# Two PSUM banks copied to SBUF ahead of their additions, and the row statistics cut into smaller, earlier pieces, in a spectral-attention kernel

## The chip, the cores and the metric

One core of one Trainium2 chip. The time is device microseconds of one execution: 1813.44 us before the change, the median of three runs (1812.06 to 1814.43). All traces are of single profiled executions.

## The reference

Four layers follow one another on x (1 x 2048 x 512, fp32), each with a layer norm ahead and a residual; both attentions have the same weights.

```
x = A_x
x = x + _A_ref(_layernorm(x, axis=-1), A_dft_seq_re, A_dft_seq_im, A_dft_hid_re, A_dft_hid_im)
x = x + _B_ref(_layernorm(x, axis=-1), B_wq, B_wk, B_wv, B_wo, B_beta)
x = x + _A_ref(_layernorm(x, axis=-1), A_dft_seq_re, A_dft_seq_im, A_dft_hid_re, A_dft_hid_im)
x = x + _B_ref(_layernorm(x, axis=-1), B_wq, B_wk, B_wv, B_wo, B_beta)
```

The spectral layer computes y = Cr (xn Dr) - Ci (xn Di) with DFT matrices of 2048 x 2048 and 512 x 512. The attention splits the sequence into four segments of 512 rows and 32 heads of width 16: causal softmax within the segment, plus a read of a memory (M, z) that the segments before have filled, mixed by a gate and multiplied by wo.

## The kernel before, in words

**Stages.** The rows lie in 16 tiles of 128 rows. Spectral 1 runs to about 373 us of the trace and overlaps the start of attention 1; attention 1 ends, and spectral 2 begins, near 740 us; attention 2 takes the end. fp32 precision is reached by splitting every operand into a high and a low part (`split`, L92: ACT writes the high part `chi`, DVE subtracts to get `clo`), and each product is three matmuls, high x high, high x low, low x high (`matmul3`, L104).

**Transform one of the spectral layer** multiplies the sequence matrix by xn. It is cut into seven products named P1 to P7 per column block `tcn`, by which sums of blocks are reused. `product(tcn, name)` (L497) accumulates eight steps k into two PSUM banks `m0` and `m1` (each 128x512), and then adds or copies the banks into blocks `c` in SBUF: DVE's additions are line L520, ACT's copies L518. What each product adds is in `TERMS`: P6 is subtracted from three blocks, P5 added to two, P3 to one. In spectral 1 (`direct`), P6, P5 and P3 take turns, one step each, for tcn 1, 2 and 3, so that six banks are in use by the products; the next tcn's first matmuls need banks that the last one's additions have freed. PSUM has eight banks in one pool ("bank"). All operands of a step come from a ring of loads (`cring`, `craw`, `v_all`), are added where needed (L407, L444, L457) and split (L96 on ACT, L98 on DVE).

**Statistics of rows.** A layer norm needs mean and variance of each row (`moments`: bn_stats L132, bn_aggr L133) and then 1/sqrt(var + eps). That is a chain over three engines: `ve` on DVE (L143), a power on POOL (`r`, L145), and four small DVE instructions (`rt` three times and `row_r`, L150 to L153; `row_scale`). The normalised tile is `xn` (L166). `measure(s, i, xr)` (L199) does this for a row tile whose sum a layer has just finished, the chain for all four tiles of a segment together, after the fourth.

**The attention's `prep(s, n)`** (L679) loads two row tiles, norms and transposes them on TensorE (`xnT`). For the last segment the statistics aren't known from `measure`, so it does them itself (`row_stats`, then `row_scale`), three slots ahead of the first `xn`. In the attention DVE's largest work is the custom instruction L827, which adds the mask to the score tile `nat` and takes each row's maximum (`junk`, `mx`); TensorE's `nat`, `sT`, `pv_bank`, `pqk`, `pvv` and `po` are scores, transposed scores, values and projections.

**Spectral 2** (not `direct`) normalises its 16 tiles in pairs at slots listed by hand in `ln_at`; each pair ends in `xa` splits (L96, L98). For its last four tiles the statistics are made in `normalise` itself. `negate` (L642) then writes `minus`, -1/std of all 16 tiles, which `add_rows` (L253) needs.

**What sets the order.** Every step is a generator that is placed by hand at numbered slots (`place(order, gen, *at)`); the slots run in order, and within a slot by `order`. TensorE's instructions, ACT's high parts and bn_stats stand in program order; the rest is put in order by a scheduler's timeline when the program is built. Each engine then works through its own list in that order, waiting where an instruction's input isn't there. DMAs are issued from SP's list and, for some stores, ACT's.

Of the kernel before, what the change touches and what calls it, by code (L numbers as in the profile page):

```python
# [10 lines left out]
F32 = mybir.dt.float32  # L11
F32R = mybir.dt.float32r
BF16 = mybir.dt.bfloat16
AF = mybir.ActivationFunctionType
ALU = mybir.AluOpType
# [3 lines left out]
P = 128  # L19
S, D, H = 2048, 512, 32  # L20
DH = D // H
NSEG = 4
L = S // NSEG
NT = S // P
DT = D // P
TC = S // 512
LT = L // P
# [29 lines left out]
def spectral_infini_kernel(  # L57
# [13 lines left out]
    V, A, G, T = nc.vector, nc.scalar, nc.gpsimd, nc.tensor  # L71

    consts = ctx.enter_context(tc.tile_pool(name="consts", bufs=1))
    sb = ctx.enter_context(tc.tile_pool(name="sb", bufs=1))
# [55 lines left out]
    def moments(mv, xt):  # L130
        st = sb.tile([P, 6], F32, name="st", bufs=2)
        pin(V.bn_stats(st, xt))  # L132
        V.bn_aggr(mv, st)  # L133
# [6 lines left out]
    def inverse_roots(mv):  # L140
        n = mv.shape[1]
        ve = sb.tile([P, LT], F32, name="ve", bufs=3)[:, :n]
        V.tensor_scalar_add(ve, mv[:, :, 1], EPS)  # L143
        r = sb.tile([P, LT], F32, name="r", bufs=3)[:, :n]
        G.tensor_tensor(out=r, in0=ve, in1=half_neg[:, :n], op=ALU.pow)  # L145
        return ve, r

    def row_scale(rr, ve, r):
        t = sb.tile([P, LT], F32, name="rt", bufs=2)[:, : rr.shape[1]]
        V.tensor_tensor(out=t, in0=r, in1=r, op=ALU.mult)  # L150
        V.tensor_tensor(out=t, in0=t, in1=ve, op=ALU.mult)
        V.tensor_scalar(t, t, -0.5, 1.5, op0=ALU.mult, op1=ALU.add)
        V.tensor_mul(rr, r, t)  # L153
# [30 lines left out]
    def place(order, gen, *at):  # L184
        for t in itertools.chain(*at):
            slots.setdefault(t, []).append((order, gen))
# [9 lines left out]
    row_r = consts.tile([P, NT], F32, name="row_r")  # L196
    minus = consts.tile([P, NT], F32, name="minus")

    def measure(s, i, xr):  # L199
        moments(row_mv[:, s * LT + i], xr)  # L200
        if i == LT - 1:
            done = slice(s * LT, (s + 1) * LT)
            row_scale(row_r[:, done], *inverse_roots(row_mv[:, done]))

    def place_spectral(x_in, x_out, t0, end, ln_at, direct):
        xa, xb, xs, us, wdt, c, right, plain = ({} for _ in range(8))
# [259 lines left out]
        def block(tcn, j):  # L466
            c[tcn, j] = t = pair("c", "ut" if tcn < 2 else "wd", 8, F32)
            return t
# [28 lines left out]
        def product(tcn, name):  # L497
            ps = [bank(f"m{m}") for m in range(2)]
            for k in range(HALF):
                t = right[tcn, name, k]  # L500
                for m in range(2):
                    matmul3(
                        ps[m],
                        lambda h: left(name, k, h, m),
                        lambda h: t[h],
                        k == 0,
                        k == HALF - 1,
                    )
                if k < HALF - 1:
                    yield  # L510
            for j, base, _ in TERMS[name]:
                if base != j:
                    block(tcn, j)
            for m in range(2):
                for j, base, op in TERMS[name]:
                    dst = c[tcn, j][:, m]
                    if base is None:
                        A.activation(dst, ps[m], AF.Copy)  # L518
                    else:
                        V.tensor_tensor(out=dst, in0=c[tcn, base][:, m], in1=ps[m], op=op)  # L520
            yield

        def chained(tcn):
# [78 lines left out]
        t = start  # L602
        if direct:
            place(2, contract(0), run_from(t, 4 * HALF, 2))
            for k in range(HALF):
                place(3, read_plain(0, k), [t + 8 * k + d for d in (-12, -4, 1, 4)])
                place(3, change_rows(k), [t + 8 * k + d for d in (5, 9)])
            t += 8 * HALF
            names = "P1", "P2", "P7", "P4"
            for tcn in range(1, TC):  # L610
                for n, name in enumerate(names):
                    place(2, product(tcn, name), run_from(t + n, HALF, 4))
                for k in range(HALF):
                    place(3, read_all(tcn, k), [t + 4 * k + d for d in (-11, -6, -4, -2, -1)])
                t += 4 * HALF
            for k in range(HALF):
                place(3, join_rows(k), [t + 5 * k + d for d in (-33, -27)])
            for tcn in range(1, TC):
                for n, name in enumerate(CHAIN):
                    place(2, product(tcn, name), run_from(t + n, HALF, 3))  # L620
                for k in range(0, HALF, 2):
                    place(3, read_rest(tcn, k), [t + 3 * k + d for d in (-12, -6, -3, 0)])
                t += 3 * HALF
        else:
            SOLO = 1
            phases = [(("P1",), range(SOLO)), (("P1", "P7"), range(SOLO, TC)), (("P7", "P2", "P4"), range(SOLO)), (("P2", "P4"), range(SOLO, TC))]
            for names, tcns in phases:
                n = len(names)
                for tcn in tcns:
                    for j, name in enumerate(names):  # L630
                        place(2, product(tcn, name), run_from(t + j, HALF, n))
                    for k in range(HALF):
                        u = t + n * k
                        if n == 1:
                            place(3, read_one(tcn, k, "P1"), [u - 9, u - 4])
                        else:
                            first = n - 2
                            if first:
                                place(3, read_added(tcn, k), [u + d for d in (-10, -6, -4)])
                            place(3, read_pair(tcn, k, names[first:]), [u + first + d for d in (-10, -6, -4, -3)])  # L640
                    t += n * HALF
            def negate():  # L642
                V.tensor_scalar(minus, row_r, -1.0, None, op0=ALU.mult)
                yield

            place(3, negate(), [t - 50])
            for k in range(HALF):
                place(3, add_rows(k), [t - 48 + 6 * k, t - 44 + 6 * k])
            for tcns in (0, 1), (2, 3):
                at = {tcn: [] for tcn in tcns}  # L650
                for name, tcn in itertools.product(CHAIN, tcns):
                    at[tcn] += run_from(t, HALF)
                    for k in range(HALF):
                        place(3, read_one(tcn, k, name), [t + k + d for d in (-9, -4)])
                    t += HALF
                for tcn in tcns:
                    place(2, chained(tcn), at[tcn])
        for k in range(2 * DT):
            cc, d = k // DT, k % DT
            tag = "craw" if k < 2 else ("chi", "clo")[k % 2]  # L660
            t = end - 7 + k if k < 2 else end - 3 + (k - 2) // 2
# [13 lines left out]
    def place_attention(x_in, x_out, t0, w_at, out_at):  # L675
# [3 lines left out]
        def prep(s, n):  # L679
            xt = [load_rows(x_in[s * LT + i]) for i in n]  # L680
            yield
            mine = slice(s * LT + n[0], s * LT + n[-1] + 1)
            mv, rr = row_mv[:, mine], row_r[:, mine]
            if s == NSEG - 1:
                ve, r = row_stats(xt, mv)
            yield
            if s == NSEG - 1:
                row_scale(rr, ve, r)
            for j, i in enumerate(n):
                with behind_max():  # L690
                    xn = normal(xt[j], mv[:, j], rr[:, j : j + 1])
                yield
                if i == 0:
                    xT[s] = sb.tile([P, 2, DT, 512], F32R, name="xT", bufs=1)
                pt = bank("xnT", (P, DT, P))
                for d in range(DT):
                    T.transpose(pt[:, d], xn[:, d * P : (d + 1) * P], ident)
                sl = slice(i * P, (i + 1) * P)
                split(xT[s][:, 0, :, sl], xT[s][:, 1, :, sl], pt)
                if j + 1 < len(n):  # L700
                    yield
            yield
# [477 lines left out]
        for n in range(NSEG * USEG):  # L1180
            t = t0 + SU * n
# [5 lines left out]
        for s in range(NSEG):  # L1187
            b = t0 + SS * s
            for j in range(2):
                t = b - (43, 51, 60, 60)[s] + 5 * j  # L1190
                first = (8, 5, 3)
                place(2, prep(s, (2 * j, 2 * j + 1)), [*(t - d for d in first), t, t, t + 2])
            place(2, values(s), *([light(b - 20), light(b)] if s else [run_from(b - 18, 8), light(b - 10)]))
            place(2, alloc_out(s), [b - 13])
# [14 lines left out]
            for g in range(NG):  # L1209
                t = b + SG * g  # L1210
# [25 lines left out]
    a2 = b1 + LB - 18  # L1236
    b2 = a2 + TC * 7 * HALF + LEAD

    def w_at(b):
# [7 lines left out]
    place_attention(mids[0], mids[1], b1, w_at(b1), lambda k: b1 + LB + 11 + k // 2)  # L1247
    place_spectral(
        mids[1], mids[2], a2, b2 - LEAD,
        [((2 * j, 2 * j + 1), a2 + t) for j, t in enumerate((-40, -24, -8, 2, 24, 34, 46, 54))],  # L1250
        False,
    )
    place_attention(mids[2], out_tiles, b2, w_at(b2), lambda k: b2 + LB + 8 + k)
# [83 lines left out]
```

## Time and profile before

| | |
|---|---|
| time, median of 3 runs | 1813.44 us |
| profiled execution, its own time | 1812.16 us |
| its span, first to last instruction | 1810.4 us |
| mean granted TensorE clock | 0.994 |
| busy: TensorE, DVE, ACT, POOL | 96%, 78%, 62%, 26% |

A row of the timeline reads: start in us from the span's start, duration in us, engine, line, operation, output<-inputs with shapes, how many of the kind follow one another without a gap, and in brackets how long the engine stood idle before it and what ended that. A row of the windows gives the busy time of each engine within a stretch and the granted clock in it (PEclk, 1.00 is full speed). PEld is TensorE's weight load, which lies beside its matmuls.

### The profile page before, as it was taken

What the parts mean: (1) busy time and instruction counts of PE and PEld (TensorE: products, weight loads), DVE (VectorE), ACT (ScalarE), POOL (GpSimd) and SP (SyncE); (2) the same over time, 40 slices, a digit from 0 to 9 for tenths busy, and PEclk for the clock granted to TensorE, in tenths of its full rate; (3) what the DMA queues carried; (4) which work ended last, traced back from release to release, by engine and by line L of the source; (5) the groups of instructions that cost most, each with busy time, mean ns of one, the idle gap of its engine ahead of it and who ended that gap; (6) DMA issues with size and microseconds to landing.
All of it is one profiled execution on the core that took longest, in us unless ns stands there. A gap on an engine that the chain in (4) does not pass through costs nothing.

```text
span 1810.4 us, 32184 instructions
## 1 busy us (share of the span) xinstructions
PE 1745.1 (96%) x10192; PEld 1260.2 (70%) x10192; DVE 1404.3 (78%) x4233; ACT 1116.3 (62%) x2391; POOL 475.7 (26%) x797
## 2 busy tenths in 40 slices
PE   7999999999999999999999999999998999999998
PEld 6888777877556666665578788888875666666654
DVE  8888987764877878878877997667658788787785
ACT  3334443432877878778764765444338887867785
POOL 1000000013443445355520000000134443534442
PEclk9999999999999999999999999999999999999999
DMA  8787765355443543444566876644545344344341
GB/s 279 245 274 236 249 228 169 116 168 175 137 151 108 156 127 123 138 127 132 164 205 203 275 231 221 195 147 153 170 136 179 124 138 144 116 138 139 103 130 42
DMA packets 169498, 302.81 MB, mean 167 GB/s; under 512 B 19568, under 2 KB 70768, under 8 KB 169328
## 3 DMA queue, kind: packets, MB, share of 16 engines
q1 hardware_dynamic: 159152, 287.39, 50.0%
q10 hardware_dynamic: 10176, 13.37, 2.0%
q8 instruction: 80, 1.31, 0.3%
q14 instruction: 90, 0.74, 0.1%
HBM read 211.83 MB, written 88.08 MB: 166 GB/s over the span
## 4 chain that ended last, share of the span: by engine, by line
PE 82%; DVE 10%; DMA 3%; issue 2%; ACT 2%; POOL 0%; SPq 0%; ACTq 0%; DVEq 0%; POOLq 0%
PE m L82 25%; PE pqk L82 9%; PE y L82 8%; PE pv_bank L82 8%; PE sT L82 7%; PE nat L82 6%; PE u L82 5%; PE pvv L82 4%; PE po L82 4%; DVE junk L827 3%; DVE c L520 1%; DVE clo L98 1%; PE on L82 1%; PE pm L82 1%; PE pM L82 1%
## 5 line engine op out<-in xcount | busy, mean ns | idle before, releaser
L827 DVE CUSTOM_DVE_ANT_0 junk<-nat,mask 128x512 bf16<-128x512 f32 (+3 forms) x1024 | 496.8, 485 | 159.6 <-PE nat L82 124.7
L896 ACT ACTIVATE pT<-sT 128x512 f32<-128x512 f32 x640 | 372.1, 599 | 14.7 <-DVE sT L893 1.4
L899 POOL TENSOR_SCALAR_AFFINE_SELECT pT<-pT 128x256 f32<-128x256 f32 (+1 forms) x448 | 199.1, 458 | 470.5 <-ACT pT L896 364.1
L82 PE MATMUL m<-chi,xa 128*128 128x512 f32 x1056 | 309.9, 394 | 5.6 <-ACT chi L96 2.7
L82 PE MATMUL sT<-stkq,stkk 99*128 99x256 bf16 (+3 forms) x1024 | 248.7, 304 | 3.9 <-ACT pT L896 1.6
L82 PE MATMUL nat<-stkk,stkq 96*128 96x512 bf16 (+3 forms) x1024 | 244.9, 300 | 6.8 <-DVE mx L827 3.4
L82 PE MATMUL m<-clo,xa 128*128 128x512 f32 x720 | 232.8, 396 | 4.1 <-DVE clo L98 4.1
L895 ACT ACTIVATE sT<-sT 128x256 f32<-128x256 f32 (+1 forms) x628 | 204.6, 336 | 49.3 <-PE sT L82 47.2
L82 PEld LDWEIGHTS m<-chi,xa 128*128 128x128 f32 x1056 | 198.7, 189 | 49.2 <-ACT chi L96 3.6
L82 PE MATMUL y<-wdt,us 128*128 128x512 f32 x768 | 182.3, 391 | 0.2 <-DVE wdt L98 0.2
L82 PEld LDWEIGHTS <-stkk 99*128 99x128 bf16 x1024 | 81.4, 98 | 132.1 <-issue 118.7
L82 PEld LDWEIGHTS y<-wdt,us 128*128 128x128 f32 x768 | 143.4, 188 | 30.4 <-DVE wdt L98 0.9
L82 PEld LDWEIGHTS m<-clo,xa 128*128 128x128 f32 x720 | 135.8, 189 | 36.2 <-DVE clo L98 8.3
L96 ACT ACTIVATE chi<-cring 128x512 fp32r<-128x512 f32 (+1 forms) x138 | 100.0, 728 | 95.7 <-PE m L82 42.6
L82 PE MATMUL pv_bank<-pT,v_all 128*17 128x128 f32 (+3 forms) x2048 | 154.0, 437 | 1.3 <-POOL pT L899 1.3
L145 POOL TENSOR_TENSOR r<-ve,half_neg 128x2 f32<-128x2 f32 (+2 forms) x24 | 19.4, 810 | 481.5 <-DVE ve L143 478.6
L82 PEld LDWEIGHTS <-stkq 96*128 96x128 bf16 x1024 | 94.1, 99 | 60.1 <-issue 19.0
L82 PE MATMUL pvv<-wv,xT 128*128 128x512 f32 x384 | 127.3, 443 | 3.7 <-DVE mx L827 3.7
L82 PE MATMUL pqk<-xT,wq 128*128 128x512 f32 x384 | 129.8, 447 | 0.0
L82 PE MATMUL po<-wo,oh 128*128 128x512 f32 x384 | 123.2, 436 | 3.1 <-DVE mx L827 2.2
L82 PE MATMUL pqk<-xT,wk 128*128 128x512 f32 x384 | 123.5, 430 | 0.0
L82 PEld LDWEIGHTS pv_bank<-pT,v_all 128*17 128x17 f32 x2048 | 53.5, 97 | 90.1 <-issue 83.9
(194 smaller groups left out, 2997.3 us busy)
## 6 DMA issues: line engine op xcount, KB each, us to landing
cring<-in_ct SPq DMA_DIRECT2D x97, 256.0 KB
stkq<-scrq SPq DMA_DIRECT2D x64, 384.0 KB
stkk<-scrk SPq DMA_DIRECT2D x64, 384.0 KB
cring<-sum SPq DMA_DIRECT2D x95, 256.0 KB
xt<-mid SPq DMA_DIRECT2D x64, 256.0 KB
cring<-in_ct SPq DMA_DIRECT2D x27, 512.0 KB
mid<-xr SPq DMA_DIRECT2D x48, 256.0 KB
scrq<-parts SPq DMA_DIRECT2D x32, 384.0 KB
```

The source lines that it names most:

```text
L82: return tc.keep_in_program_order(op(*args, **kwargs))
L96: pin(A.activation(hi, src, AF.Copy, scale=scale))
L98: lo_engine.tensor_tensor(out=lo, in0=src, in1=hi.bitcast(F32), op=ALU.subtract)
L145: G.tensor_tensor(out=r, in0=ve, in1=half_neg[:, :n], op=ALU.pow)
L520: V.tensor_tensor(out=dst, in0=c[tcn, base][:, m], in1=ps[m], op=op)
L827: last_max[0] = V.tensor_tensor_reduce(junk[:, :n], src, mask[:, 512 - n :], 1.0, 3e38, ALU.add, ALU.min, dst,)
L895: A.activation(blocks, blocks, AF.Relu)
L896: A.activation(dst, ps, AF.Exp, scale=-SCALE)
L899: G.affine_select(blocks, blocks, pattern=[[0, n] for n in blocks.shape[1:-1]] + [[1, P]], compare_op=ALU.is_ge, fill=0.0, base=0, channel ...
```

## The change

Five edits:

1. In transform one of spectral 1, for tcn 1 and 2 and the products P6 and P5, ACT copies both banks into SBUF tiles `kept`, and DVE's additions read `kept` and not the banks: two places in the program with four copies each.
2. `measure` runs the chain of `row_scale` for segment 0 after every two tiles, not after four.
3. `negate` is cut in two: twelve tiles at t - 60 and four at t - 36 (before: all at t - 50).
4. `prep` of the last segment has one more step (the chain apart from the first `xn`) and starts 4 slots earlier.
5. Three of spectral 2's times of `normalise` are 2, 2 and 4 slots later.

```diff
     def measure(s, i, xr):
         moments(row_mv[:, s * LT + i], xr)
-        if i == LT - 1:
-            done = slice(s * LT, (s + 1) * LT)
+        step = LT // 2 if s == 0 else LT
+        if i % step == step - 1:
+            done = slice(s * LT + i + 1 - step, s * LT + i + 1)
             row_scale(row_r[:, done], *inverse_roots(row_mv[:, done]))
...
+            held = ps
+            if direct and tcn < TC - 1 and name in ("P6", "P5"):
+                held = [
+                    sb.tile([P, 512], F32, name="kept", tag="praw", bufs=2) if name == "P6"
+                    else sb.tile([P, 768], F32, name="kept", tag="parts", bufs=2)[:, :512]
+                    for _ in range(2)
+                ]
+                for m in range(2):
+                    A.activation(held[m], ps[m], AF.Copy)
+                pass
             for m in range(2):
                 for j, base, op in TERMS[name]:
                     dst = c[tcn, j][:, m]
                     if base is None:
-                        A.activation(dst, ps[m], AF.Copy)
+                        A.activation(dst, held[m], AF.Copy)
                     else:
-                        V.tensor_tensor(out=dst, in0=c[tcn, base][:, m], in1=ps[m], op=op)
+                        V.tensor_tensor(out=dst, in0=c[tcn, base][:, m], in1=held[m], op=op)
...
-            def negate():
-                V.tensor_scalar(minus, row_r, -1.0, None, op0=ALU.mult)
+            def negate(some):
+                V.tensor_scalar(minus[:, some], row_r[:, some], -1.0, None, op0=ALU.mult)
                 yield
-            place(3, negate(), [t - 50])
+            place(3, negate(slice(0, NT - LT)), [t - 60])
+            place(3, negate(slice(NT - LT, NT)), [t - 36])
...
             if s == NSEG - 1:
                 row_scale(rr, ve, r)
+                yield
...
-                first = (8, 5, 3)
+                first = (12, 10, 6, 3) if s == NSEG - 1 else (8, 5, 3)
...
-        [((2 * j, 2 * j + 1), a2 + t) for j, t in enumerate((-40, -24, -8, 2, 24, 34, 46, 54))],
+        [((2 * j, 2 * j + 1), a2 + t) for j, t in enumerate((-40, -24, -8, 2, 24, 36, 48, 58))],
```

TensorE's instructions stand in the same order before and after. After the diff the line numbers are higher: L98 and L166 stay, L520 becomes L531, L827 L840, L643 L654.

Three places on DVE show how the rest moves. The first is the end of transform two in spectral 1 and the first `prep` of attention 1. In these rows `st` and `row_mv` are the statistics of a row tile, `xr` a finished row tile, `us` a split of transform two, and the rows with `xt` as input are the normalised tiles 0, 1 and 2 (in the second fence 0 and 1). Before:

```order
L132 BN_STATS st_3131<-xr_3082 128x6
L151 TENSOR_TENSOR rt_3073<-rt_3073,ve_3069 128x4
L133 BN_AGGR row_mv_111<-st_3131 128x2
L152 TENSOR_SCALAR rt_3073<-rt_3073 128x4
L153 TENSOR_TENSOR row_r_112<-r_3071,rt_3073 128x4
L166 TENSOR_SCALAR xn_3114<-xt_3025,row_mv_111,row_r_112 128x512
L166 TENSOR_SCALAR xn_3181<-xt_3027,row_mv_111,row_r_112 128x512
L166 TENSOR_SCALAR xn_3231<-xt_3116,row_mv_111,row_r_112 128x512
L170 TENSOR_TENSOR xr_3135<-y_3134,xr_3135 128x512
```

After:

```order
L150 TENSOR_TENSOR rt_2977<-r_2975 128x2
L151 TENSOR_TENSOR rt_2977<-rt_2977,ve_2973 128x2
L152 TENSOR_SCALAR rt_2977<-rt_2977 128x2
L153 TENSOR_TENSOR row_r_112<-r_2975,rt_2977 128x2
L166 TENSOR_SCALAR xn_3139<-xt_3050,row_mv_111,row_r_112 128x512
L166 TENSOR_SCALAR xn_3206<-xt_3052,row_mv_111,row_r_112 128x512
L170 TENSOR_TENSOR xr_3042<-y_3041,xr_3042 128x512
L98 TENSOR_TENSOR wq_3103<-raw_3054,wq_3103 128x512
L98 TENSOR_TENSOR us_3120<-c_1338,us_3120 128x256
```

The chain covers two tiles and stands, with both `xn`, 17 rows earlier, ahead of the splits and of the sums of row tiles 2 and 3.

The second place is the `prep` of the last segment in attention 1 (attention 2 has the same). `junk,mx` are maxima of score tiles, `xn` tiles 12 and 13, `pkn` and `state0` the memory's update. Before:

```order
L151 TENSOR_TENSOR rt_7880<-rt_7880,ve_7822 128x2
L1064 TENSOR_TENSOR pkn_7856<-pM_7922,same_head_2512 128x136
L827 ISA junk_7920,mx_7759<-nat_7915,mask_2507 128x384
L827 ISA mx_7759 128x1
L152 TENSOR_SCALAR rt_7880<-rt_7880 128x2
L1071 TENSOR_TENSOR state0_4319<-state0_4319,pkn_7856 128x136
L827 ISA junk_7948,mx_7759<-nat_7946,mask_2507 128x512
L827 ISA mx_7759 128x1
L153 TENSOR_TENSOR row_r_112<-r_7824,rt_7880 128x2
L166 TENSOR_SCALAR xn_7885<-xt_7743,row_mv_111,row_r_112 128x512
L166 TENSOR_SCALAR xn_7966<-xt_7745,row_mv_111,row_r_112 128x512
```

After:

```order
L143 TENSOR_SCALAR ve_7875<-row_mv_111 128x2
L98 TENSOR_TENSOR oh_7901<-oT_7896,oh_7901 128x512
L840 ISA junk_7927,mx_7803<-nat_7922,mask_2515 128x256
L840 ISA mx_7803 128x1
L166 TENSOR_SCALAR xn_7933<-xt_7690,row_mv_111,row_r_112 128x512
L840 ISA junk_7942,mx_7803<-nat_7940,mask_2515 128x512
L840 ISA mx_7803 128x1
L150 TENSOR_TENSOR rt_7984<-r_7877 128x2
L1077 TENSOR_TENSOR pkn_7909<-pM_7966,same_head_2520 128x136
```

The first `xn` stands ahead of four maxima that stood ahead of it before; its own chain stands about 40 rows higher (between the maxima in which DVE had its last gap), and the `ve` and `rt` seen here are those of tiles 14 and 15.

The third place is the last `normalise` of spectral 2 (tiles 14 and 15), within transform one. `chi` and `clo` are the split operands of the products, in TensorE's order. Before:

```order
L143 TENSOR_SCALAR ve_11628<-row_mv_111 128x2
L150 TENSOR_TENSOR rt_11668<-r_11630 128x2
L151 TENSOR_TENSOR rt_11668<-rt_11668,ve_11628 128x2
L152 TENSOR_SCALAR rt_11668<-rt_11668 128x2
L153 TENSOR_TENSOR row_r_112<-r_11630,rt_11668 128x2
L166 TENSOR_SCALAR xn_11673<-xt_11562,row_mv_111,row_r_112 128x512
L166 TENSOR_SCALAR xn_11678<-xt_11564,row_mv_111,row_r_112 128x512
L643 TENSOR_SCALAR minus_113<-row_r_112 128x16
L98 TENSOR_TENSOR xa_11675<-xn_11673,xa_11675 128x512
L98 TENSOR_TENSOR xa_11680<-xn_11678,xa_11680 128x512
L98 TENSOR_TENSOR chi_11683<-cring_10482,chi_11683 128x512
```

After (the rows from `chi_11692` on to the block; `chi_11692` is the counterpart of `chi_11683`):

```order
L98 TENSOR_TENSOR chi_11692<-cring_10516,chi_11692 128x512
L458 TENSOR_TENSOR craw_11074<-craw_11074,cring_10516 128x512
L531 TENSOR_TENSOR c_11702<-c_11689,m1_11513 128x512
L132 BN_STATS st_11705<-xt_11640 128x6
L98 TENSOR_TENSOR clo_11715<-cring_10516,clo_11715 128x512
L98 TENSOR_TENSOR chi_11728<-cring_10516,chi_11728 128x512
L445 TENSOR_TENSOR craw_11074<-craw_11074,craw_11075 128x512
L98 TENSOR_TENSOR clo_11742<-craw_11074,clo_11742 128x512
L458 TENSOR_TENSOR cring_10516<-cring_10516,craw_11075 128x512
L133 BN_AGGR row_mv_111<-st_11705 128x2
L132 BN_STATS st_11708<-xt_11642 128x6
L133 BN_AGGR row_mv_111<-st_11708 128x2
```

The block from `ve` to the second `xa` follows right behind these rows: it now stands behind four operands of the products (`chi_11692`, `clo_11715`, `chi_11728`, `clo_11742`) that stood behind it before.

## The prediction

> **What bounds the kernel now.** I read the page's busy times first, then the waits of TensorE (PE), then the timeline around each long wait, then the windows' granted clock.
>
> ```profile
> span 1810.4 us, 32184 instructions
> PE 1745.1 (96%) x10192; PEld 1260.2 (70%) x10192; DVE 1404.3 (78%) x4233; ACT 1116.3 (62%) x2391; POOL 475.7 (26%) x797
> ```
>
> PE is busy for 96% of the span, and the change leaves its instructions as they are. So only two things can go: PE's idle 65 us, and time in which its clock is throttled. The waits of PE (total us, times, longest) say whom it waits for:
>
> ```profile
> PE xnT L82 <- DVE xn L166: 10.2, 7, 2.2
> PE m L82 <- DVE clo L98: 4.1, 5, 1.9
> PE m L82 <- ACT chi L96: 2.7, 1, 2.7
> PE m L82 <- DVE c L520: 2.1, 2, 1.6
> ```
>
> The first, third and fourth rows are the waits that the five edits touch: norms that come late, a product operand behind a norm, and banks that DVE hasn't freed. Placed in time:
>
> ```profile
> 274.07 0.61 PE L82 MATMUL m<-chi,xa 128*128 128x512 f32 x1 [1.60 <-DVE c L520]
> 309.30 0.50 PE L82 MATMUL m<-chi,xa 128*128 128x512 f32 x1 [0.46 <-DVE c L520]
> 373.65 0.63 PE L82 MATMUL xnT<-ident,xn 128*128 128x128 f32 x4 [1.82 <-DVE xn L166]
> 720.58 0.63 PE L82 MATMUL xnT<-ident,xn 128*128 128x128 f32 x4 [2.16 <-DVE xn L166]
> 1003.43 0.49 PE L82 MATMUL m<-chi,xa 128*128 128x512 f32 x1 [2.73 <-ACT chi L96]
> 1004.33 2.16 PE L82 MATMUL m<-chi,xa 128*128 128x512 f32 x5 [0.40 <-DVE chi L98]
> 1607.86 0.63 PE L82 MATMUL xnT<-ident,xn 128*128 128x128 f32 x4 [2.15 <-DVE xn L166]
> ```
>
> These stalls sum to 11.32 us. Behind four of them the clock falls; the column after POOL's busy time is the granted clock:
>
> ```profile
> 274.00:278.00 4.00, 3.93 (x10) 3.10 (x11) 3.34 (x6) 1.06 (x1) 0.00 (x0) 0.57 0.70 245
> 373.00:377.00 4.00, 3.35 (x17) 2.88 (x18) 2.40 (x5) 0.64 (x2) 0.00 (x0) 1.00 0.58 202
> 721.00:725.00 4.00, 4.00 (x21) 2.34 (x23) 3.97 (x12) 2.57 (x5) 2.36 (x3) 0.57 0.73 229
> 1003.00:1008.00 5.00, 4.17 (x11) 3.04 (x12) 5.00 (x10) 5.00 (x10) 0.00 (x0) 0.68 0.70 230
> 1608.00:1613.00 5.00, 5.00 (x31) 2.67 (x34) 4.93 (x15) 2.57 (x5) 2.46 (x3) 0.66 0.69 223
> ```
>
> A clock of 0.57 over 4 us loses 0.43 x 4 = 1.7 us of work; the other windows give 1.7 (721), 1.6 (1003) and 1.7 (1608). So a stall of about 2 us can cost nearly twice its length. Not each does: behind the 1.82 at 373.65 the clock stays 1.00. By the Trainium skill, page "TensorE: Matmul & The Clock Gate", "Why this matters for your kernels", a drop comes from idle gaps over about 3 us; "What's actually happening" says that the activity window is 3413 ns long and free-running. The drops behind 1.6 to 2.7 us here contradict the first figure; by it the clock would give nothing here (the first rival below has that time).
>
> **The kept banks (transform one of spectral 1, two places).** At the first, DVE does ten additions from banks, with splits between them; ACT idles:
>
> ```profile
> 265.68 4.87 DVE L520 TENSOR_TENSOR c<-c,m 128x512 f32<-128x512 f32 x8
> 271.60 0.69 DVE L520 TENSOR_TENSOR c<-c,m 128x512 f32<-128x512 f32 x1
> 273.33 1.89 DVE L520 TENSOR_TENSOR c<-c,m 128x512 f32<-128x512 f32 x3
> 267.20 1.07 ACT L96 ACTIVATE chi<-v_all 128x1024 fp32r<-128x1024 f32 x1 [2.69 <-DMA sum<-craw]
> 275.99 1.06 ACT L96 ACTIVATE chi<-v_all 128x1024 fp32r<-128x1024 f32 x1 [6.42 <-DMA v_all<-in_ct]
> L518 ACT ACTIVATE c<-m x14: 576/598/601, 138.4 to 996.7; 128x512 f32<-128x512 f32 x14
> 275.12 0.70 DVE L407 TENSOR_TENSOR v_all<-v_all,cring 128x512 f32<-128x512 f32 x1
> ```
>
> P6 has three additions per bank and P5 two, so P5's second bank is free only after the tenth (the first of the 273.33 row, which ends about 273.33 + 0.6), and PE's next product waits 1.60 for it. With four copies of 0.60 (the L518 row) by ACT, which stands idle 2.69 us before 267.20, the four banks are free near 269, and the 1.60 is gone. The additions don't get cheaper: an addition from SBUF takes 0.70 (L407) against 0.69. DVE's list is unchanged there and was in time by little, so PE, no longer held, meets the next `clo` sooner: those splits come one or two additions apart, and I book 0.95 us of new waits for them. The fourth copy stands behind the `chi` of 267.20, and delays the next `chi` by about 0.4, within that. Net 0.65 of stall and, with that stall, the 1.7 of clock: 2.35. At the second place little is to be had:
>
> ```profile
> 302.05 4.87 DVE L520 TENSOR_TENSOR c<-c,m 128x512 f32<-128x512 f32 x8
> ```
>
> DVE begins its additions there close behind P6's last matmul, so the first now waits for a copy of 0.60: DVE, and the splits queued behind these additions, come up to 0.6 later (I take 0.45). The bank wait of 0.46 goes, later splits cost PE about 1.0, and it loses 0.5. Together -1.85 us; between +0.5 (the copy delays both places, no clock returns) and -3.3 (1.60 and the clock).
>
> **Row statistics by halves.** Ahead of 373.65 DVE works off sums, a split and bn_stats before the chain's end and `xn`:
>
> ```profile
> 371.76 0.69 DVE L132 BATCH_NORM_STATS2 st<-xr 128x6 f32<-128x512 f32 x1
> 372.96 1.00 DVE L166 TENSOR_SCALAR xn<-xt,row_mv,row_r 128x512 f32<-128x512 f32 x2
> ```
>
> In the new order both `xn` of tiles 0 and 1 stand 17 rows earlier, ahead of the third tile's sum. `xnT` finds them, and 1.82 goes: -1.8 us (between -1.0, if the displaced splits come late for `y`, and -1.8). Three more chains cost a POOL power and four small DVE rows each; the nearest row is the same chain in attention 1:
>
> ```profile
> 647.95 0.58 DVE L150 TENSOR_TENSOR rt<-r 128x4 f32<-128x4 f32 x1 [0.62 <-POOL r L145]
> ```
>
> While DVE waits in that row, the score maxima stand behind it. Most of that lies under PE's work; I book +0.3 in all (0 to 0.9).
>
> **The first `prep` of the last segment, in both attentions.** DVE's rows in attention 1:
>
> ```profile
> 706.55 0.42 DVE L827 CUSTOM_DVE_ANT_0 junk<-nat,mask 128x256 bf16<-128x256 f32 x1 [2.63 <-PE nat L82]
> 710.75 0.69 DVE L132 BATCH_NORM_STATS2 st<-xt 128x6 f32<-128x512 f32 x1
> 715.82 0.69 DVE L827 CUSTOM_DVE_ANT_0 junk<-nat,mask 128x512 bf16<-128x512 f32 x1
> 719.88 1.00 DVE L166 TENSOR_SCALAR xn<-xt,row_mv,row_r 128x512 f32<-128x512 f32 x2
> 703.90 0.64 POOL L899 TENSOR_SCALAR_AFFINE_SELECT pT<-pT 128x512 f32<-128x512 f32 x1 [2.03 <-ACT pT L896]
> ```
>
> The statistics of 710.75 to 719.88 move into the idle 2.63 us ahead of 706.55; POOL's power stands behind the select of 703.90 and so starts at once. `xn` moves ahead of the maximum of 715.82 and is done near 716.4, where PE asks for it at 720.58 - 2.16 = 718.42. The stall goes, and the clock's 1.7: up to 3.86. What is late next is DVE, which fills all of 721 to 725 (3.97 of 4.00): PE, ahead of it by 3.9 us, will wait for maxima. I give back 1.36: -2.5 us each, -5.0 for both (between -1.0 and -3.86 each). SP's list also moves: the load of a row tile (`xr`) goes ahead of two stores of `scrq`, and may hold them until `xn` frees its buffer.
>
> ```profile
> 715.73 1.67 SPq L776 DMA_DIRECT2D scrq<-parts  x2
> 736.65 0.32 SPq L798 DMA_DIRECT2D stkq<-scrq  x1
> ```
>
> From 715.73 to `xn` at 716.4 that is 0.7 us, or 4 us if the buffer is the one that frees last; the next read of scores' operands is 21 us behind the stores, so I book nothing (beyond about 15 us PE would wait for `stkq`).
>
> **Spectral 2's last norms.**
>
> ```profile
> 999.35 0.18 DVE L143 TENSOR_SCALAR ve<-row_mv 128x2 f32<-128x2 f32 x1
> 1003.59 0.69 DVE L98 TENSOR_TENSOR chi<-cring,chi 128x512 fp32r<-128x512 f32 x1
> 1007.20 0.69 DVE L457 TENSOR_TENSOR cring<-cring,craw 128x512 f32<-128x512 f32 x1
> 1011.28 1.52 PE L82 MATMUL m<-chi,xa 128*128 128x512 f32 x6
> ```
>
> From 999.35 to 1003.59 the norm block keeps DVE from products: 4.24 us, and PE stalls 2.73 + 0.40. The block now stands four products later, and DVE has both to do in either order: block and the seven product rows (1003.59 to 1007.80) end at about 1007.8. So PE is stalled not at 1000.70 (1003.43 - 2.73) but at the fifth product. Four products of at most 1.52 (six matmuls, the 1011.28 row) bring it there by 1006.8, its operand, split behind 1007.8, is there near 1008.5, and before it started this product at 1011.28. That is 2.8 us ahead; a new stall of some 2 us would lose a window again (1.6): -1.2 us. The range is from +1.0 (the operands behind come late as well) to -4.7 (2.73 + 0.40 + 1.6). The later slots hold up nothing: the products don't need these rows yet. `negate` in two rows costs 0.2 us on DVE, within that.
>
> **Sum.** -1.85 - 1.8 + 0.3 - 5.0 - 1.2 = -9.55 us. The profiled execution took 1812.16 us (1.76 outside its span), so 1802.6. The median before, 1813.44, is 1.28 above that execution; I put that back, because the clock's losses differ by execution: **1804.0 us**.
>
> **Rivals.**
> - *The stalls go, the clock doesn't come back*, since other stalls of 1.5 to 3 us take the place (the 1.82 at 373.65 lost nothing, the 1.60 at 274.07 lost 1.7, so length alone doesn't decide). The terms 1.7 and 2 x 1.7 are gone: 1804.0 + 5.1 = 1809.1. For: 373.65. Against: the four windows above. By the 3 us of the Trainium skill's page "TensorE: Matmul & The Clock Gate" only the stalls would count as well.
> - *DVE is the bound* in the attentions: PE's lead is given back in full, and what stays is the 1.8 at 373.65 and 0.65 at 274: 1813.44 - 2.45 = 1811.0. For: DVE 3.97 of 4.00 at 721. Against: the 2.63 idle us that take the statistics.
> - *Slower*: a statistics block holds PE up at its new place. DVE works in order; a block of `ve` to `xa` or `xn` takes up to 4.24 us, and where PE's lead over DVE is less than that, PE waits for the difference. Six blocks are added or moved (three halves, two `prep`, one `normalise`). The break-even is 9.55 / 6 = 1.6 us each; at 3 us each the time is 1804 + 18 = 1822. Against: three of the six lie at DVE's idle times.
> - *Nothing*: the waits only move on to the next instruction, 1813.
>
> **Chances.** Forecast 0.55 (1798 to 1808.5), clock 0.18, DVE 0.15, slower 0.07, nothing 0.05. Below 0.2% (3.6 us, about what a measurement can tell) counts as the same, so faster is below 1809.8: 0.55, two thirds of the second and a third of the third, 0.72; the same 0.21; slower 0.07. The range takes in the second and third cases and the low bounds of the terms in part: 1797 to 1812.5; all of the low bounds together (-3.3, -1.8, -7.7, -4.7) would be 1796.
>
> **What would show it.** At 274 no `c` wait, and `kept` rows of 0.60; at 374, 718 and 1605 `xnT` with no `xn` wait and a clock of 1.00 behind; a single stall near 1006 to 1008 in place of that at 1003. I am wrong if PE's waits for maxima (`mx`) in 706 to 740 grow by over 2 us, if a clock loss stays at 721, or if `clo` waits at 266 to 280 exceed 1.6.

## The result, and the profile after

The changed kernel took 1804.46 us (median of 4 runs, 1801.35 to 1806.06) against 1813.58 before (4 runs, 1812.06 to 1814.43): ratio 0.9947, 95% interval 0.9928 to 0.9966. That is 9.1 us less; 1804.0 was forecast. The total agrees, in part by luck: of its terms one was too low, and two don't show in the runs of their own edits, as the runs below tell.

The page after:

```profile
span 1804.2 us, 32200 instructions
PE 1746.6 (97%) x10192; PEld 1262.5 (70%) x10192; DVE 1406.4 (78%) x4249; ACT 1119.2 (62%) x2399; POOL 477.7 (26%) x800
```

The waits of TensorE after:

```profile
PE m L82 <- DVE clo L98: 6.4, 8, 1.9
PE xnT L82 <- DVE xn L166: 4.1, 4, 1.4
PE mT L82 <- DVE mx L840: 3.3, 4, 1.9
PE m L82 <- ACT chi L96: 2.6, 1, 2.6
```

The wait for `c` is gone and `xnT` waits 6.1 us less, but `clo` has grown by 2.3 and `mT` by 1.3 us. Where that lies, the timeline says:

```profile
275.12 0.50 PE L82 MATMUL m<-clo,xa 128*128 128x512 f32 x1 [0.42 <-DVE clo L98]
281.75 0.50 PE L82 MATMUL m<-clo,xa 128*128 128x512 f32 x1 [0.51 <-DVE clo L98]
309.66 0.50 PE L82 MATMUL m<-clo,xa 128*128 128x512 f32 x1 [0.42 <-DVE clo L98]
312.00 0.50 PE L82 MATMUL m<-clo,xa 128*128 128x512 f32 x1 [0.68 <-DVE clo L98]
373.26 0.60 PE L82 MATMUL xnT<-ident,xn 128*128 128x128 f32 x4
715.88 0.60 PE L82 MATMUL xnT<-ident,xn 128*128 128x128 f32 x4
843.03 0.27 PE L82 MATMUL mT<-ident_b,mparts 128*80 128x128 bf16 x1 [1.88 <-DVE mx L840]
1005.25 0.49 PE L82 MATMUL m<-chi,xa 128*128 128x512 f32 x1 [2.55 <-ACT chi L96]
1006.14 2.07 PE L82 MATMUL m<-chi,xa 128*128 128x512 f32 x4 [0.40 <-DVE chi L98]
```

Both `xnT` rows have no bracket: the forecast's stalls there are gone. Four small `clo` waits stand where the bank waits were, one long stall stands at 1005, and the wait at 843, 0.72 us in the trace before, is now 1.88, which nobody forecast. The windows with the granted clock (behind POOL's column):

```profile
238.00:242.00 4.00, 4.00 (x12) 3.15 (x11) 4.00 (x6) 0.09 (x1) 0.00 (x0) 0.57 0.80 246
275.00:279.00 4.00, 3.82 (x15) 2.85 (x16) 4.00 (x7) 0.00 (x0) 0.00 (x0) 1.00 0.54 160
716.00:720.00 4.00, 4.00 (x48) 2.41 (x46) 3.97 (x11) 3.71 (x8) 2.66 (x4) 1.00 0.90 283
842.00:850.00 8.00, 6.97 (x26) 5.02 (x27) 5.50 (x25) 4.14 (x11) 5.22 (x9) 0.57 0.25 85
1006.00:1010.00 4.00, 3.85 (x10) 3.10 (x11) 3.87 (x8) 4.00 (x8) 0.00 (x0) 0.57 0.69 204
1392.00:1399.00 7.00, 6.20 (x25) 3.10 (x27) 4.92 (x19) 4.06 (x9) 1.45 (x3) 0.52 0.59 186
```

The clock stays full behind 275 and 716, as forecast, and is lost at 238, 842 and 1392, where it was full in the trace before. TensorE's instructions stand in one order in both kernels, so the start of the same instruction can be subtracted, after less before (times of the trace before, us):

```
place                           248    278    339    399    519    700    730    822    852    972   1003   1033   1395   1426   1577   1638
TensorE's start, after-before  +3.28  +0.29  +1.57  -0.44  -2.65  -2.39  -6.32  -6.36  -2.08  -2.68  -6.34  -3.66  -4.23  -1.74  -1.77  -5.72
```

The steps read off it: kept banks -2.99 (248 to 278) and +1.28 (to 339); halves -2.01; the two preps -3.93 and -3.95 (1577 to 1638); the norms -3.66 and +2.68 (972 to 1033). The rest (+3.28 up to 248, -2.21 up to 519, +4.28 at 852, +2.49 at 1426, and smaller steps) isn't from a term of the forecast. Whether it comes from the change, the repeated run and the other traces tell.

### The profile page after: what moved, and what is told of

It is laid out like the page before. It is cut to its first block, busy times and chain, and to the rows that moved or that the text cites. A ratio compares the mean times of both kernels' runs of the same rounds, so it can differ in the third digit from the quotient of the medians.

```text
span 1804.2 us, 32200 instructions
## 1 busy us (share of the span) xinstructions
PE 1746.6 (97%) x10192; PEld 1262.5 (70%) x10192; DVE 1406.4 (78%) x4249; ACT 1119.2 (62%) x2399; POOL 477.7 (26%) x800
## 4 chain that ended last, share of the span: by engine, by line
PE 75%; DVE 8%; ACT 2%; issue 2%; DMA 1%; POOL 0%; ACTq 0%; DVEq 0%; SPq 0%
PE m L82 21%; PE y L82 9%; PE pqk L82 9%; PE pv_bank L82 8%; PE sT L82 7%; PE nat L82 6%; PE pvv L82 4%; PE po L82 4%; DVE junk L840 3%; PE pm L82 1%; PE pM L82 1%; PE on L82 1%; DVE c L531 1%; ACT pT L909 1%; PE oT L82 1%
## 5 line engine op out<-in xcount | busy, mean ns | idle before, releaser
L840 DVE CUSTOM_DVE_ANT_0 junk<-nat,mask 128x512 bf16<-128x512 f32 (+3 forms) x1024 | 496.6, 485 | 152.2 <-PE nat L82 116.3
L82 PE MATMUL pv_bank<-pT,v_all 128*17 128x512 f32 (+3 forms) x2048 | 152.6, 434 | 0.8 <-POOL pT L912 0.8
```

The lines of the kernel that those rows point to most:

```text
L82: return tc.keep_in_program_order(op(*args, **kwargs))
L840: last_max[0] = V.tensor_tensor_reduce(junk[:, :n], src, mask[:, 512 - n :], 1.0, 3e38, ALU.add, ALU.min, dst,)
```

## The experiments

The theory was the forecast's: each edit takes away a stall and the clock lost behind it, in the sizes of the sum. Rivals: the clock's losses come and go by chance; DVE gives the gain back. Eleven runs were made: ten further kernels, and the changed one again. They came in three groups; a group shares a chip and its runs of before, whose median was 1810.92 (30 runs), 1814.81 (11) and 1813.17 us (17). On one chip, runs of before spread over 8 to 11 us. So differences under 2 us are read from traces, not medians.

**Each edit alone.** The kept banks alone (the diff's second part on the kernel before):

```diff
+            held = ps
+            if direct and tcn < TC - 1 and name in ("P6", "P5"):
...
-                        V.tensor_tensor(out=dst, in0=c[tcn, base][:, m], in1=ps[m], op=op)
+                        V.tensor_tensor(out=dst, in0=c[tcn, base][:, m], in1=held[m], op=op)
```

> Only the kept banks, all else as before. The forecast's term: 1.85 us faster than before, no wait for c (L520) at 274, two or three new clo waits of 0.4 to 0.7 us between 275 and 312, and the clock full behind 274. Rival (the clock's losses fall by chance of a free-running window, so on the mean only the stalls count): the bank wait of 1.60 and the 0.46 go, 2.1 us of new clo waits come, and the median is within 0.5 us of before.

Measured: 1810.17 us, ratio 0.9999 (0.9987 to 1.0010). Its TensorE waits for the same four `clo` and no more for `c`:

```profile
274.41 0.50 PE L82 MATMUL m<-clo,xa 128*128 128x512 f32 x1 [0.42 <-DVE clo L98]
281.04 0.50 PE L82 MATMUL m<-clo,xa 128*128 128x512 f32 x1 [0.52 <-DVE clo L98]
308.95 0.50 PE L82 MATMUL m<-clo,xa 128*128 128x512 f32 x1 [0.42 <-DVE clo L98]
311.29 0.50 PE L82 MATMUL m<-clo,xa 128*128 128x512 f32 x1 [0.68 <-DVE clo L98]
```

New waits sum to 2.04 us; before, 1.60, 0.46 and a `clo` wait of 0.33 sum to 2.39. The third is this row:

```profile
271.74 0.50 PE L82 MATMUL m<-clo,xa 128*128 128x512 f32 x1 [0.33 <-DVE clo L98]
```

The rival is right: 0.35 us of waits go, and the rest is the clock's chance. The 13 traces agree, if TensorE's place is followed from 248 to 339 as in the table above. With the kept banks it gains 1.64 to 1.72 us on the trace before (five traces, without the last run below). Without them it gains 1.59 to 1.61 where the window behind the bank wait kept its clock (four traces) and nothing where it was lost (before and two others). So the copies are worth 0.1 us, and 1.6 of clock more where the bank wait would have lost it, in three of seven traces.

The statistics by halves alone:

```diff
-        if i == LT - 1:
-            done = slice(s * LT, (s + 1) * LT)
+        step = LT // 2 if s == 0 else LT
+        if i % step == step - 1:
+            done = slice(s * LT + i + 1 - step, s * LT + i + 1)
```

> Only the row statistics of segment 0 by halves. The forecast's term: 1.5 us faster (1.8 for the xnT wait at 374, less 0.3 for three more chains). Rival (DVE gives it back in the attention): the xnT wait of 1.82 is gone but the waits for maxima at 640 to 650 and 1530 to 1550 grow by as much, and the time is that of before within 0.5 us.

Measured: 1810.05, ratio 0.9991 (0.9982 to 1.0000). The `xnT` wait is gone, and TensorE is 2.0 us ahead of its place before, behind 374; of that it gives back 0.3 at 640.

```profile
373.21 0.60 PE L82 MATMUL xnT<-ident,xn 128*128 128x128 f32 x4
```

The forecast's term of 1.5 holds in the trace; the runs' interval, nothing to 3.3 us, covers it.

The earlier prep alone:

```diff
                 row_scale(rr, ve, r)
+                yield
...
-                first = (8, 5, 3)
+                first = (12, 10, 6, 3) if s == NSEG - 1 else (8, 5, 3)
```

> Only the earlier prep of the last segment. The forecast's term: 5.0 us faster, with no xnT wait at 718 and 1605 and TensorE ahead of before by 2.5 to 3.9 us behind each place. Rival (clock by the window's phase): the two stalls of 2.16 go in full, and of the clock's 1.7 each only the share of executions in which a 2.2 us stall falls into one window, about half, so 4.3 + 1.7 = 6.0 less what DVE gives back. Rival (DVE the bound): under 2.5 us in all, with new waits for maxima at 720 to 740.

Measured: 1804.52 (7 runs), ratio 0.9953 (0.9935 to 0.9971), so 6.4 us by medians and 8.5 by the ratio; behind the two places TensorE gained 3.89 and 3.93 us on the trace before. The clock in its windows is full:

```profile
716.00:720.00 4.00, 4.00 (x46) 2.12 (x45) 3.97 (x11) 3.30 (x8) 2.75 (x3) 1.00 0.88 278
1602.00:1606.00 4.00, 4.00 (x40) 2.46 (x42) 3.97 (x13) 3.97 (x9) 2.67 (x4) 1.00 0.95 283
```

The four traces without this edit (before and the runs of the other three alone) all have a window of half clock behind both stalls, not behind half of them as the rival on the phase has it; here is the kept banks' run:

```profile
715.00:719.00 4.00, 1.85 (x13) 1.36 (x12) 3.96 (x12) 2.27 (x6) 1.76 (x2) 1.00 0.63 206
719.00:723.00 4.00, 4.00 (x24) 1.75 (x26) 3.96 (x12) 2.46 (x5) 2.46 (x3) 0.57 0.85 250
```

So the stall and the clock go in full, 3.9 us each place in the traces, and DVE gives nothing back: the forecast's -2.5 each was too small, and its upper bound of 3.86 was the right value. The runs' interval, 5.3 to 11.8 us, holds the traces' 7.8 and not quite the forecast's 5.0.

The later norms alone:

```diff
+            place(3, negate(slice(0, NT - LT)), [t - 60])
+            place(3, negate(slice(NT - LT, NT)), [t - 36])
...
-(-40, -24, -8, 2, 24, 34, 46, 54)
+(-40, -24, -8, 2, 24, 36, 48, 58)
```

> Only spectral 2's later norms and the negation in two parts. The forecast's term: 1.2 us faster, one stall of 2 to 3 us near 1006 in place of those at 990, 1003 and 1004, and the clock lost behind it as before. Rival (the block holds TensorE up as long at the new place): stall of 3.1 us and more, time of before within 0.5 us.

Measured: 1813.12, ratio 1.0006 (0.9996 to 1.0017). One stall for three, shorter than the rival's 3.1, but two windows of half clock behind it:

```profile
1008.38 3.39 PE L82 MATMUL m<-chi,xa 128*128 128x512 f32 x6 [2.55 <-ACT chi L96]
1008.00:1015.00 7.00, 6.52 (x15) 4.75 (x16) 6.86 (x13) 6.63 (x12) 0.00 (x0) 0.51 0.74 216
```

The stalls before include one that the prediction doesn't show:

```profile
989.76 1.43 PE L82 MATMUL m<-chi,xa 128*128 128x512 f32 x5 [0.39 <-DVE chi L98]
```

From 972 to 1033 TensorE lost 0.1 us on the trace before, which had one window of half clock there, and 0.6 more up to 1124. The stalls are 0.6 to 0.9 us shorter (2.95 in the changed kernel, 2.65 here, 3.52 before), and in this trace the clock takes that back. In four other traces with the later norms only one window is lost, and TensorE gains 0.9 to 1.3 us over that stretch: the first trace after, the repeated run, the one without the kept banks and the one with P5's additions on POOL. Two traces without the edit gain 0.5 there as well. The runs of this edit alone, for which the forecast's 1.2 lies just outside the interval (0.7 us faster to 3.1 slower), show no gain.

**The changed kernel again, and without the kept banks.** The first is the same program:

> The changed kernel once more, beside a kernel before on one chip. Forecast's theory: 9.6 us faster, as the record has it (ratio 0.9947). The trace has the same stalls as the first trace of this kernel, while the windows of half clock lie elsewhere if they depend on the phase of a free-running window: windows with over about 1.9 us of TensorE idle are followed by one at half clock, windows under 1.4 us are not. Rival (the half clock belongs to places of the program): half clock at 238, 504, 842, 1006 and 1392 again.

Measured: 1801.27 (6 runs), ratio 0.9926 (0.9908 to 0.9945). The stalls of the forecast's places are the same to 0.01 us; the stall at 843 has its length of before, and the clock at its place is full:

```profile
839.62 0.22 PE L82 MATMUL mT<-ident_b,mparts 128*80 128x128 bf16 x1 [0.72 <-DVE mx L840]
238.00:242.00 4.00, 4.00 (x15) 3.17 (x14) 4.00 (x6) 1.06 (x1) 0.00 (x0) 0.74 0.95 274
843.00:851.00 8.00, 7.54 (x66) 4.65 (x66) 7.70 (x33) 5.55 (x13) 3.22 (x7) 1.00 0.48 141
1392.00:1399.00 7.00, 7.00 (x60) 4.80 (x53) 5.74 (x29) 6.07 (x15) 2.79 (x6) 1.00 0.00 0
```

The half clock at 238 and 1005 is there again, behind stalls of 1.88 and 2.55; those at 842 and 1392 aren't. So one program has +4.28 at 852 in one execution and nothing in another, and so with +2.49 at 1426. For the two other steps the traces of all runs tell: at 248 those of the experiments lie between -0.25 and +3.13, and from 399 to 519 each gains 0.6 to 2.9 us on the trace before, whatever its edits, so +3.28 and -2.21 are such chances too.

Whether the change has a part in the loss at 852 stays open. It comes, with 4.2 to 4.4 us, in five of the eight traces of kernels that have both the halves and the earlier prep, and in none of the five others, four of which ran on one chip; so few traces can't tell whether these two edits make it likelier.

```diff
-            if direct and tcn < TC - 1 and name in ("P6", "P5"):
-                held = [
...
+                        V.tensor_tensor(out=dst, in0=c[tcn, base][:, m], in1=ps[m], op=op)
```

> The changed kernel without the kept banks. Forecast's term: 1.85 us slower than the changed kernel. What the run of the kept banks alone suggests: within 1 us of it; the bank wait of 1.6 us at 274 and of 0.46 at 309 is back, the clo waits at 275, 282, 310 and 312 (2.0 us together) are gone.

Measured: 1800.75, ratio 0.9922 (0.9904 to 0.9940), not to be told from the changed kernel beside it (1801.27). The waits of 1.60 and 0.46 are back, the four `clo` waits gone. The kept banks bring nothing that can be measured; the 0.1 us and the clock's chance, together some 0.8 on the mean (0.1 + 3/7 x 1.6, an estimate), are too small for these runs.

**Places and engines for the norm blocks.** First the last three norms earlier, then POOL for the split of the last four tiles:

```diff
-(-40, -24, -8, 2, 24, 36, 48, 58)
+(-40, -24, -8, 2, 24, 34, 41, 45)
```

> The changed kernel with spectral 2's last three norms at 34, 41 and 45 in place of 36, 48 and 58. Theory (DVE is full from 975 to 1045, so the place of the blocks only decides which product waits): one or two stalls of 2 to 3 us together between 980 and 1008, time within 1 us of the changed kernel. Rival (the blocks find DVE's free time at 955 to 975, where it is busy 11 of 20 us): no stall of over 0.5 us, TensorE 3 us and more ahead behind 1010, time 3 to 5 us less.

Measured: 1800.02, ratio 0.9922 (0.9905 to 0.9939), within 1.3 us of the changed kernel. The stall moves to 981 and is 0.6 us shorter:

```profile
981.51 0.50 PE L82 MATMUL m<-clo,xa 128*128 128x512 f32 x1 [1.92 <-ACT clo L96]
982.41 1.84 PE L82 MATMUL m<-clo,xa 128*128 128x512 f32 x5 [0.39 <-DVE clo L98]
```

The norms still stand ahead of DVE's splits there, and the place of the blocks only picks the product that waits.

```diff
-                engines = {"lo_engine": V if direct or i >= 8 else G, "hi_engine": V if leads else A}
+                engines = {"lo_engine": V if direct or 8 <= i < 12 else G, "hi_engine": V if leads else A}
```

> The changed kernel with the low parts of the normalised tiles 12 to 15 of spectral 2 written by POOL (idle there) and not by DVE. Theory (DVE is the bound at 1005): each block costs DVE 1.3 us less, the stall of 2.55 at 1005 shrinks to about 1.3, the clock isn't lost behind it, time 1.3 to 3 us less than the changed kernel. Rival (a DVE instruction beside a POOL tensor instruction waits for its end, as DVE's 0.98 us of L999 at 841 suggests): DVE loses what it saved, stall 2 us or more, time within 1 us.

Measured: 1805.79, ratio 0.9943 (0.9924 to 0.9962), 4.5 us above the changed kernel on its chip. In its trace a stall of 3.01 at 843, of which below, costs 4.4 us with its clock, and from 972 to 1033 TensorE loses 1.0 us on the repeated run. Its stall at 1005 grew to 2.85. DVE's rows beside POOL's, from its timeline:

```profile
1004.40 2.96 POOL L98 TENSOR_TENSOR xa<-xn,xa 128x512 fp32r<-128x512 f32 x2 [2.11 <-ACT xa L96]
1005.40 0.82 DVE L98 TENSOR_TENSOR chi<-craw,chi 128x512 fp32r<-128x512 f32 x1 [1.20 <-ACT chi L96]
1006.14 1.77 DVE L98 TENSOR_TENSOR clo<-craw,clo 128x512 fp32r<-128x512 f32 x1
1007.84 0.68 DVE L445 TENSOR_TENSOR cring<-cring 128x512 f32<-128x512 f32 x1
```

A `clo` split, as long as the row of 0.68 below it when it runs alone, takes 1.77 and ends 0.55 behind the second POOL instruction (1004.40 + 2.96 = 1007.36), as if it had begun only then. The rival holds: the work that went to POOL is paid again on DVE.

**The rest of the sum.** First halves and prep together on the kernel before (their two diffs above):

> Before with the row statistics by halves and the earlier prep alone: neither the kept banks nor the later norms. Theory after eight runs (these two edits carry the gain, the other two exchange one stall for another of the same length): the time of the changed kernel within 1.5 us, ratio to before 0.992 to 0.995. Rival (the forecast's terms: kept 1.85, norms 1.2): 3 us slower than the changed kernel, ratio 0.9955 and more.

Measured: 1804.33, ratio 0.9950 (0.9931 to 0.9968). That is at the edge of the theory's numbers, with an interval that covers the rival's too. These two edits give at least most of the gain; that the other two give nothing measurable rests on their own runs.

The changed kernel without the kept banks and with the early norms (the two diffs above together):

> The changed kernel without the kept banks and with the norms of spectral 2 at 34, 41 and 45. Theory: each of the two is worth under 0.7 us of stall, so within 1.5 us of the changed kernel and of the run with early norms. Rival (they add up): 2 us less than the changed kernel.

Measured: 1803.64, ratio 0.9946 (0.9927 to 0.9966); they don't add up to anything. No version beats the changed kernel by more than the spread.

P5's additions on POOL, from the kept copies:

```diff
-                        V.tensor_tensor(out=dst, in0=c[tcn, base][:, m], in1=held[m], op=op)
+                        (G if held is not ps and name == "P5" else V).tensor_tensor(out=dst, in0=c[tcn, base][:, m], in1=held[m], op=op)
```

> The changed kernel with P5's four additions per place done by POOL from the kept copies (POOL is idle there), so that DVE has 2.4 us less at each place. Theory (a DVE instruction with two SBUF inputs waits while a POOL tensor instruction runs, 1.77 us for a clo in place of 0.69 in the run with the norms on POOL): DVE's splits beside POOL's additions take up to 1.8 us, and the clo waits at 275 to 312 stay at 1.5 us and more together. Rival (POOL and DVE run side by side): the clo waits of 2.0 us go, time 2 us less than the changed kernel.

Measured: 1810.87 (12 runs), ratio 0.9986 (0.9969 to 1.0003): the gain is almost lost. The waits at 275 and 312 are 2.48 and 2.47, and DVE's rows beside POOL's additions stretch:

```profile
267.90 4.69 DVE L531 TENSOR_TENSOR c<-c,kept 128x512 f32<-128x512 f32 x4
272.51 2.28 DVE L98 TENSOR_TENSOR clo<-v_all,chi 128x1024 fp32r<-128x1024 f32 x1
274.71 2.30 DVE L98 TENSOR_TENSOR clo<-craw,chi 128x1024 fp32r<-128x1024 f32 x1
```

The splits take 2.28 where the changed kernel's take 1.22. From the first addition (266.69) to the end of the second split DVE needs 10.3 us, with POOL doing part of the additions; the changed kernel, with all of them on DVE, needs 7.8 (269.02 to 276.80).

## Why the prediction came out, point by point

- **What bounds the kernel**: right. Only TensorE's idle time and its clock moved; its list is the same.
- **Kept banks, -1.85**: the step that failed is the clock's 1.7, counted as certain. The stalls came nearly as booked: the 1.60 went, the new `clo` waits at the first place are 0.93 (0.95 was booked), and both places together gain 0.1 to 0.35 us (0.15 was booked). But the bank wait, with the 0.33 ahead of it or alone, lost a window in three of seven traces only. That the first pair of traces shows -1.71 up to 339 is luck: the trace before was one of the three. The wait passed from the bank to the next `clo`, since DVE's list of additions and splits is as long as before.
- **Halves, -1.8 + 0.3**: right, 2.0 gained in the trace and 0.3 given back.
- **Preps, -5.0**: right in mechanism, too small in size. The 1.36 given back at each place didn't come: the statistics left a stretch that DVE filled and went into its idle 2.6 us, and no new wait for maxima followed. Measured in the traces, 3.9 each.
- **Norms, -1.2**: the place was right: 1008.5 was forecast in before's time, and 1005.25 plus the lead of 2.68 at 972 is 1007.9. The forecast counted one window lost behind the new stall, and the traces with one gain 0.9 to 1.3. What it left out is the second window, which the run of this edit alone lost, and with it the gain. That run's times show none; how often the second window goes is open.
- **Sum**: -9.55 forecast. By the runs of single edits: 0 + 1.6 + 6.4 to 8.5 - 1.1 = 6.9 to 9.0, and the two measurements of the whole are 9.1 and 13.5 by medians. The preps gave some 2.8 more than booked in the traces, and banks and norms gave less, so the total isn't evidence for each term. What parts 9.1 from 13.5 is open; the loss of 4.2 to 4.4 at 852, which is in the first trace after and not in the repeated one, has that size.
- **Rivals**: the one on the clock was half right. For windows with 1.85 us and more of idle time it is wrong; for shorter stalls it is a matter of chance. DVE as the bound held for the banks and in part for the norms, but not in the attentions. *Slower* and *nothing* are out by the time, although the norms' block does hold TensorE up for 2.95 at its new place.

## What to carry to other kernels

When one engine waits for a buffer that a second, full engine frees, freeing the buffer sooner only hands the wait to the next operand from that engine; first ask which engine's list gets shorter. Moving small work into an idle gap of the full engine, as the earlier statistics did, was worth the stall in full. Price a stall with its clock window, and by its length: here the stalls of 2.15 us were paid nearly twice in all four traces that have them, the stall of 1.6 in three of seven.

## What the runs showed of the hardware

**The clock.** The half-clock stretches of a trace start on a grid of 3.41 us, whose phase differs from trace to trace. I laid that grid over all 13 traces and summed the gaps between TensorE's matmuls in each full-clock window from the first full clock to 1790 us: 0.9 to 1.45 us idle, 0 of 44 windows followed by one at half clock; 1.45 to 1.85 us, 23 of 31; 1.85 us and more, 40 of 40. So about half a window of idle time is enough, whether or not it comes in one piece: a window with gaps of 1.09 and 0.38 was followed by half clock. A stall cut by the grid's edge can escape, and so the same program loses other windows in other runs: of the runs of before on one chip, one of 1808.27 us had a mean clock of 0.996 and one of 1816.93 had 0.991. The two `xnT` stalls of 2.15 that the earlier prep takes away lie 887.3 us apart, 260 windows less 0.2 us, and so fall on the grid alike: that both lost their window in four traces is four cases, not eight. The Trainium skill, page "TensorE: Matmul & The Clock Gate", section "What's actually happening", has the length and the free phase, and these traces agree with both; the idle gap of about 3 us that the section "Why this matters for your kernels" allows is too long by these counts.

**DVE beside POOL.** The stall at 843 is 1.88 us in the first trace after, 0.72 in the second trace of the same program, about 3.0 in four of the others and 0.65 to 0.72 in the rest. In the first, short DVE instructions overlapped POOL's:

```profile
838.90 0.96 POOL L227 TENSOR_TENSOR xn<-xn 128x256 f32<-128x256 f32 x1 [0.98 <-DVE xn L166]
839.19 0.70 DVE L856 SCALAR_TENSOR_TENSOR mparts<-mx 128x16 bf16<-128x16 f32 x1
841.24 1.15 POOL L780 TENSOR_TENSOR parts<-rem,parts 128x512 bf16<-128x512 f32 x1
841.44 0.98 DVE L999 TENSOR_TENSOR rec<-rec,gate 128x16 f32<-128x16 f32 x1
```

Both end within 0.05 us of POOL's instruction. In the repeated run the same two rows take 0.17:

```profile
837.18 1.05 POOL L227 TENSOR_TENSOR xn<-xn 128x256 f32<-128x256 f32 x1 [0.98 <-DVE xn L166]
837.47 0.17 DVE L856 SCALAR_TENSOR_TENSOR mparts<-mx 128x16 bf16<-128x16 f32 x1
838.84 0.17 DVE L999 TENSOR_TENSOR rec<-rec,gate 128x16 f32<-128x16 f32 x1
```

So a DVE instruction with two SBUF inputs can wait until a POOL tensor instruction ends, as in the rows of the two POOL experiments. The 13 traces have 199 rows of L999's kind at whose start such a POOL instruction had over 0.15 us to run: they took 0.64 to 1.17, and 506 beside an idle POOL 0.16 to 0.18. A split with one input in PSUM (`oh` from `oT`) shows nothing of it, 0.67 to 0.69 in all 65 such cases. The Trainium skill, page "Trainium Architecture — The Big Picture", section "What this means for kernel authors", names an exclusive lock between DVE and GpSimd in place of a split bandwidth, and these rows agree.

But which of the two waits is not to be read from their starts. L856 starts 0.29 us behind POOL's `xn` in both traces above: in the first it takes 0.70 and POOL 0.96, in the second 0.17 and POOL 1.05. In the five traces with a long stall at 843 POOL comes first there, in the other eight DVE, and what decides it isn't in the trace. Where POOL comes first, the rows behind are late and meet more of POOL's, so that one program differs by 1.2 us of stall between the two traces and, with the clock, by 4.3 us at 852.
